# One 512-column product in place of two of 256 in a full expert slot, and a sum behind it

## The chip, the cores and the metric

The kernel runs on one core of one Trainium2 chip. The metric is the device time of one execution in microseconds (us); a measurement is the median of several runs. The engines are TensorE (PE; its weight loads are listed apart as PEld), VectorE (DVE), ScalarE (ACT), GpSimd (POOL) and SyncE (SP). Each works through its own list of instructions in order and waits where a semaphore tells it to.

## What is computed

The reference is a local attention with summary keys, followed by a mixture of experts in which each token goes to the one expert with the largest gate. Only the second part matters here (3072 tokens, width D = 512, E = 8 experts, hidden width F = 1024):

```python
e_idx = np.argmax(x @ w_gate, axis=1)
for e in range(E):
    mask = e_idx == e
    h = np.maximum(x[mask] @ w1[e], 0.0)
    ye = h @ w2[e]
    out[mask] = gate_w[mask, None] * eom[mask, e, None] * ye
```

## The kernel before

**Tiling.** Tokens are gathered by expert into slots of 256 rows (a full slot) or 128 (a half slot). Slot 0 is worked among the last of the attention, slot 1 by `full_with` while DVE still works out the table of the remaining slots, the others by `full` and `half`. There are 11 full slots of the kind that the change touches (slot 1, then seven in a row, then three that alternate with three half slots).

**Precision.** Products run on float32r operands. To keep float32 accuracy, each operand is split into a high part (rounded to float32r) and a low part (the rest), and a product is three: high by high, high weights by low rows, low weights by high rows. ACT makes high parts, DVE subtracts to make low parts. This holds for the weights (`split_w`, L868 and L869, on 128x512 tiles; sixteen tiles of w1 and w2 for each slot), for the rows (`take_x`, L883 and L884) and for the hidden layer (L902 and L903).

**A full slot.** `first(j)`, for j = 0 to 7, makes 128 of the 1024 hidden columns: for each of four chunks c of D, three products of 256 columns into one PSUM tile `hp` (L899 to L901), so 96 products for a slot. ACT then writes `hh`, the high part of relu(hp) (L902), and DVE `hl`, the low part (L903). The PSUM tiles alternate between two tags of two banks each ("S" and "PT"), so `hp` of j+4 reuses the bank of j. `second` makes the output with 48 products of 512 columns (L1082 to L1084, six in each block j); ahead of block 4, `take_x` transposes the rows of the next slot (L881) and splits them (L883, L884). The rows are in `xh` and `xl`, two tiles apart; the weights of the next slot are split into place as soon as the tile that they replace has been used.

**Order.** In the attention and in slot 1 every engine keeps the order in which the program is written (`manual_schedule(engines=ALL)`). In slot 1, each `first(j)` is followed on DVE by up to three small steps of the slot table (`next(rest)`, L728 to L760 and L640 to L688) and by one split of a weight tile; the loop over the second blocks then goes on with splits, and with `take_x` ahead of block 4 (`full_with`, L990 to L1018). From slot 2 on only POOL has the written order; for the others the framework chooses one when the program is built, by its own estimate of times.

Of the kernel before, what the change touches and what calls it, by code (L numbers as in the profile page):

```python
# [11 lines left out]
F32 = mybir.dt.float32  # L12
F32R = mybir.dt.float32r
BF16 = mybir.dt.bfloat16
I32 = mybir.dt.int32
AF = mybir.ActivationFunctionType
ALU = mybir.AluOpType
# [5 lines left out]
P = 128  # L23
# [8 lines left out]
PB = {"S": 2, "PT": 2, "PV": 2, "TR": 1, "MS": 1}  # L32
# [16 lines left out]
NC = DM // P  # L49
NF = F // P  # L50
SLOT = 256
# [209 lines left out]
def attention(tc, const, sa, sb, st, ps, dr, q, k, v, id_sb, c_sb, wg_sb, x_dr, l_dr, rt, moe, table, begin, swap):  # L261
# [240 lines left out]
    def route(b):  # L502
# [15 lines left out]
        yield  # L518
        first = tmp("first", [P, TB])
        nc.vector.tensor_reduce(out=first, in_=fi, axis=AX.X, op=ALU.min)  # L520
        yield
        oh = tmp("oh", sh)
# [246 lines left out]
class Experts:  # L769
# [17 lines left out]
    def open_first(self, pool):  # L787
        self.pool1, self.mp, self.mp2 = pool, pool.__enter__(), None
        self.wt = {1: [self.fixed(self.mp, f"w1{x}", NF, [P, 512], dt) for x, dt in (("h", F32R), ("l", F32))]}
        self.xg = self.fixed(self.mp, "xg", 2, [P, DM], F32)  # L790
        self.xh, self.xl = (self.mp.tile([P, NC, SLOT], dt, name=f"xhl{i}", tag=f"xhl{i}", bufs=1)
                            for i, dt in enumerate((F32, F32R)))
        for t in self.xg:
            self.tc.nc.gpsimd.memset(t, 0.0)
        self.wt[2] = [self.fixed(self.mp, f"w2{x}", NF // 2, [P, 512], F32R) for x in "hl"]

    def open_second(self, pool):
        self.pool2, self.mp2 = pool, pool.__enter__()
        for x, made in zip("hl", self.wt[2]):
            made += self.fixed(self.mp2, f"w2{x}_", NF // 2, [P, 512], F32R)  # L800
# [90 lines left out]
    def first(self, j, hidden, nxt, tag):  # L891

        nc = self.tc.nc
        hh, hl = hidden
        hp = self.ps.tile([P, SLOT], F32, name="hp", tag=tag, bufs=PB[tag])
        fs = slice((j % 4) * P, (j % 4) * P + P)
        for c in range(NC):
            w_h, w_l = (x[4 * (j // 4) + c] for x in self.wt[1])
            nc.tensor.matmul(hp, lhsT=w_h[:, fs], rhs=self.xh[:, c, :], start=c == 0, stop=False)  # L899
            nc.tensor.matmul(hp, lhsT=w_h[:, fs], rhs=self.xl[:, c, :], start=False, stop=False)  # L900
            nc.tensor.matmul(hp, lhsT=w_l[:, fs], rhs=self.xh[:, c, :], start=False, stop=c == NC - 1)  # L901
        nc.scalar.activation(hh[:, j, :], hp, AF.Relu)  # L902
        nc.vector.scalar_tensor_tensor(hl[:, j, :], hp, 0.0, hh[:, j, :].bitcast(F32), ALU.max, ALU.subtract)  # L903
        if j % 4 == 3:
            self.fetch_w(1, nxt, range(j - 3, j + 1))

# [74 lines left out]

    def early_x(self, c):
        if c == 0:
            self.xh = self.mp.tile([P, NC, SLOT], F32R, name="xhl0", tag="xhl0", bufs=1)
        self.take_x(2, (c,))

    def early_write(self):
# [32 lines left out]
    def half(self, s, nxt_n=2):  # L1020
# [31 lines left out]
        with self.tc.manual_schedule(engines={mybir.EngineType.PE}):  # L1052
            first(0, range(4))
            relu(0)
            first(1, range(SPLIT))
            turn(0)
            first(1, range(SPLIT, 4))
            relu(1)
            self.fetch_w(1, nxt, range(4))
            yp.append(ps.tile([P, DM], F32, name="yp0", tag="PV", bufs=PB["PV"]))  # L1060
            for j in range(NF):
                if j == XAT and nxt in self.slots:
                    self.take_x(nxt_n)
                    self.fetch(s + 2, 2)
                self.second_block(j, yp, hh, hl)
                if j == TAT:
                    turn(1)
                    self.fetch_w(1, nxt, range(4, 8))
                if j < NF - 1:
                    if j >= 2:  # L1070
                        self.fetch_w(2, nxt, [j - 2])
                else:
                    with self.tc.manual_schedule(engines={mybir.EngineType.PE, mybir.EngineType.DVE}):
                        self.write(s, yp)
                        self.fetch_w(2, nxt, [j - 2, j - 1, j])
# [110 lines left out]
```

## Time and profile before

| | us |
|---|---|
| median of three runs | 521.12 (520.93 to 524.67) |
| the profiled execution, as a run | 519.98 |
| the profiled execution, its span (first to last instruction) | 517.8 |
| PE busy in that span | 479.9 |
| DVE busy | 363.7 |
| ACT busy | 319.8 |

An engine's busy time is a sum over stages with different limits. A row of a timeline gives the start, the duration, the engine, the line and the tiles; `[0.50 <-ACT hh L902]` at its end says that the engine sat idle for 0.50 us before it, until that instruction was done. Matmuls overlap: a product is listed with some 0.28 us, while the next starts 0.12 us after it. What a product costs is therefore the distance from one start to the next.

### The profile page before, as it was taken

How to read it: one execution, taken by the hardware profiler on the slowest of the kernel's cores; microseconds unless marked ns; L12 is line 12 of the kernel's file. 1: busy time of each engine (PE TensorE's matmuls, PEld its weight loads, DVE VectorE, ACT ScalarE, POOL GpSimd, SP SyncE). 2: the span in 40 equal slices, each digit the busy share in tenths (PEclk: the TensorE clock that was granted, in tenths of full speed). 3: DMA queues.
4: the chain of work that ended last, by engine and by line, in shares of the span. 5: the costliest groups of instructions: out<-in, count | busy, mean ns of one | idle time of the engine just before them, and what ended most of it. 6: DMA issues, size and time to landing. Idle time of an engine off the chain costs nothing.

```text
span 517.8 us, 12814 instructions
## 1 busy us (share of the span) xinstructions
PE 479.9 (93%) x4486; PEld 409.3 (79%) x4486; DVE 363.7 (70%) x802; ACT 319.8 (62%) x633; POOL 229.3 (44%) x257
## 2 busy tenths in 40 slices
PE   6877999979988999999999999999999989989992
PEld 6756677667656788989899898989899869869871
DVE  2748767979886679895757666574757678668674
ACT  3475679577766876555556555463756567567573
POOL 8353556457796615845235131322315315415212
PEclk9997999999999999999999999999999999999998
DMA  9999929999128379728574949476674966967952
GB/s 220 192 231 189 251 67 260 247 255 227 44 86 271 94 221 384 280 72 299 176 268 170 324 137 312 146 265 197 218 237 168 303 207 245 311 209 246 300 193 82
DMA packets 108283, 111.40 MB, mean 215 GB/s; under 512 B 42878, under 2 KB 70110, under 8 KB 108208
## 3 DMA queue, kind: packets, MB, share of 16 engines
q1 hardware_dynamic: 99488, 91.75, 60.1%
q0 software_dynamic: 8720, 18.73, 11.7%
q8 instruction: 37, 0.61, 0.5%
q14 instruction: 38, 0.31, 0.2%
HBM read 98.70 MB, written 15.15 MB: 220 GB/s over the span
## 4 chain that ended last, share of the span: by engine, by line
PE 73%; DVE 6%; ACT 5%; DMA 5%; issue 4%; SPq 3%; POOL 1%; DVEq 0%; ACTq 0%; POOLq 0%
PE yp L1084 9%; PE yp L1083 9%; PE yp L1082 9%; PE hp L901 8%; PE hp L899 8%; PE hp L900 8%; PE pv L447 3%; PE sp L400 3%; PE hp L964 3%; PE pt L432 3%; PE xp L881 2%; PE ms L323 2%; DMA raw<-in_moe_w_dram 2%; DVE pr L410 2%; DMA raw_q<-in_q_dram 2%
## 5 line engine op out<-in xcount | busy, mean ns | idle before, releaser
L869 DVE TENSOR_TENSOR w2l<-raw,w2h 128x512 fp32r<-128x512 f32 x128 | 84.9, 688 | 41.0 <-ACT w2h L868 40.4
L868 ACT ACTIVATE w2h<-raw 128x512 fp32r<-128x512 f32 x128 | 78.0, 628 | 55.8 <-PE yp L1084 23.7
L901 PE MATMUL hp<-xhl,w1l 128*128 128x256 f32 x352 | 99.4, 283 | 0.0
L900 PE MATMUL hp<-xhl,w1h 128*128 128x256 f32 x352 | 99.4, 283 | 0.0
L899 PE MATMUL hp<-xhl,w1h 128*128 128x256 f32 x352 | 99.0, 283 | 0.0
L832 POOL DMA_INDIRECT xg<-x_dr,lst x34 | 40.4, 1188 | 120.0 <-PE xp L881 109.2
L1082 PE MATMUL yp<-w2h,hh 128*128 128x512 f32 x216 | 86.6, 401 | 0.0
L1084 PE MATMUL yp<-w2h,hl 128*128 128x512 f32 x216 | 85.0, 394 | 0.0
L1083 PE MATMUL yp<-w2l,hh 128*128 128x512 f32 x216 | 85.0, 393 | 0.0
L869 DVE TENSOR_TENSOR w1l<-raw,w1h 128x512 fp32r<-128x512 f32 x117 | 75.3, 693 | 8.6 <-ACT w1h L868 7.3
L868 ACT ACTIVATE w1h<-raw 128x512 fp32r<-128x512 f32 x120 | 67.3, 621 | 6.8 <-DMA raw<-in_moe_w_dram 5.2
L900 PEld LDWEIGHTS hp<-xhl,w1h 128*128 128x128 f32 x352 | 67.4, 191 | 0.9
L899 PEld LDWEIGHTS hp<-xhl,w1h 128*128 128x128 f32 x352 | 67.2, 191 | 1.0
L901 PEld LDWEIGHTS hp<-xhl,w1l 128*128 128x128 f32 x352 | 67.4, 192 | 0.0
L902 ACT ACTIVATE hh<-hp 128x256 fp32r<-128x256 f32 x88 | 33.5, 381 | 51.9 <-PE hp L901 49.8
L903 DVE SCALAR_TENSOR_TENSOR hl<-hp,hh 128x256 fp32r<-128x256 f32 x88 | 36.1, 420 | 35.2 <-ACT hh L902 35.1
L422 POOL TENSOR_TENSOR pr<-pr,mn 128x960 f32<-128x960 f32 x24 | 43.4, 1811 | 35.4 <-DVE mn L417 14.2
L1107 POOL DMA_INDIRECT out_dram<-y,lst x27 | 31.3, 1159 | 56.7 <-DVE y L1104 29.2
L1084 PEld LDWEIGHTS yp<-w2h,hl 128*128 128x128 f32 x216 | 40.5, 188 | 8.8
L1082 PEld LDWEIGHTS yp<-w2h,hh 128*128 128x128 f32 x216 | 40.7, 188 | 8.1
L1083 PEld LDWEIGHTS yp<-w2l,hh 128*128 128x128 f32 x216 | 40.7, 188 | 7.8
L278 ACT ACTIVATE pT<-pt 120x512 f32<-120x512 f32 x48 | 27.2, 595 | 26.7 <-PE pt L432 26.5
(202 smaller groups left out, 843.3 us busy)
## 6 DMA issues: line engine op xcount, KB each, us to landing
raw<-in_moe_w_dram SPq DMA_DIRECT2D x248, 256.0 KB, 5.1
raw_k<-in_k_dram SPq DMA_DIRECT2D x12, 512.0 KB, 7.9
raw_q<-in_q_dram SPq DMA_DIRECT2D x12, 512.0 KB, 5.5
vw<-in_v_dram SPq DMA_DIRECT2D x44, 128.0 KB, 6.5
x_dr<-xs POOLq DMA_DIRECT2D x17, 256.0 KB, 4.3
vw<-in_v_dram SPq DMA_DIRECT2D x33, 64.0 KB, 4.5
w1l<-in_moe_w_dram SPq DMA_DIRECT2D x8, 256.0 KB, 3.4
x_dr<-xs SPq DMA_DIRECT2D x7, 256.0 KB, 3.9
```

What stands on the lines that cost most here:

```text
L422: nc.gpsimd.tensor_tensor(pr, pr, mns.pop(i).unsqueeze(2).to_broadcast([P, H, W]), ALU.subtract)
L832: nc.gpsimd.indirect_dma_start(out=self.xg[t], out_offset=None, in_=self.x_dr[0:rows, :], in_offset=bass.IndirectOffsetOnAxis(ap=self.list ...
L868: nc.scalar.activation(hi, raw, AF.Copy)
L869: (lo_by or nc.vector).tensor_tensor(lo, raw, hi.bitcast(F32), ALU.subtract)
L899: nc.tensor.matmul(hp, lhsT=w_h[:, fs], rhs=self.xh[:, c, :], start=c == 0, stop=False)
L900: nc.tensor.matmul(hp, lhsT=w_h[:, fs], rhs=self.xl[:, c, :], start=False, stop=False)
L901: nc.tensor.matmul(hp, lhsT=w_l[:, fs], rhs=self.xh[:, c, :], start=False, stop=c == NC - 1)
L902: nc.scalar.activation(hh[:, j, :], hp, AF.Relu)
L903: nc.vector.scalar_tensor_tensor(hl[:, j, :], hp, 0.0, hh[:, j, :].bitcast(F32), ALU.max, ALU.subtract)
L1082: nc.tensor.matmul(y, lhsT=hh[:, j, tk], rhs=w_h, start=j == 0, stop=False)
L1083: nc.tensor.matmul(y, lhsT=hh[:, j, tk], rhs=w_l, start=False, stop=False)
L1084: nc.tensor.matmul(y, lhsT=hl[:, j, tk], rhs=w_h, start=False, stop=j == NF - 1)
```

## The change

In a full slot the rows' high and low parts lie side by side in one tile (`x[:, c, 0, :]` and `x[:, c, 1, :]`), and the high weights meet both in one product of 512 columns, which fills the whole bank: half 0 collects high by high, half 1 high weights by low rows. The product of the low weights with the high rows (256 columns) is added to half 1. The bank's halves are then added: ACT copies half 1 to a new SBUF tile `lo`, DVE adds half 0 to it, and the relu (ACT) and the subtraction (DVE) read `lo` instead of PSUM. The written order (`first`, then the table's steps, then the split) is not changed. Slot 0 and the half slots keep their products.

```diff
-        self.xh, self.xl = (self.mp.tile([P, NC, SLOT], dt, name=f"xhl{i}", tag=f"xhl{i}", bufs=1)
-                            for i, dt in enumerate((F32, F32R)))
+        self.rows(F32)
...
+    def rows(self, dt):
+        self.x = self.mp.tile([P, NC, 2, SLOT], dt, name="xhl", tag="xhl", bufs=1)
+        self.xh, self.xl = self.x[:, :, 0, :], self.x[:, :, 1, :]
...
-        hp = self.ps.tile([P, SLOT], F32, name="hp", tag=tag, bufs=PB[tag])
+        hp = self.ps.tile([P, 2, SLOT], F32, name="hp", tag=tag, bufs=PB[tag])
...
-            nc.tensor.matmul(hp, lhsT=w_h[:, fs], rhs=self.xh[:, c, :], start=c == 0, stop=False)
-            nc.tensor.matmul(hp, lhsT=w_h[:, fs], rhs=self.xl[:, c, :], start=False, stop=False)
-            nc.tensor.matmul(hp, lhsT=w_l[:, fs], rhs=self.xh[:, c, :], start=False, stop=c == NC - 1)
-        nc.scalar.activation(hh[:, j, :], hp, AF.Relu)
-        nc.vector.scalar_tensor_tensor(hl[:, j, :], hp, 0.0, hh[:, j, :].bitcast(F32), ALU.max, ALU.subtract)
+            nc.tensor.matmul(hp.rearrange("p a n -> p (a n)"), lhsT=w_h[:, fs], rhs=self.x[:, c].rearrange("p a n -> p (a n)"),
+                             start=c == 0, stop=False)
+            nc.tensor.matmul(hp[:, 1, :], lhsT=w_l[:, fs], rhs=self.xh[:, c, :], start=False, stop=c == NC - 1)
+        lo = self.mp2.tile([P, SLOT], F32, name="lo", bufs=2)
+        nc.scalar.activation(lo, hp[:, 1, :], AF.Copy)
+        nc.vector.tensor_tensor(lo, hp[:, 0, :], lo, ALU.add)
+        nc.scalar.activation(hh[:, j, :], lo, AF.Relu)
+        nc.vector.scalar_tensor_tensor(hl[:, j, :], lo, 0.0, hh[:, j, :].bitcast(F32), ALU.max, ALU.subtract)
...
-            self.xh = self.mp.tile([P, NC, SLOT], F32R, name="xhl0", tag="xhl0", bufs=1)
+            self.rows(F32R)
```

## Rows read from the trace of the kernel before

**Rows 1.** The page's first part: busy time of each engine, its share of the span, and its instructions.

```profile
PE 479.9 (93%) x4486; PEld 409.3 (79%) x4486; DVE 363.7 (70%) x802; ACT 319.8 (62%) x633; POOL 229.3 (44%) x257
```

**Rows 2.** Busy time of each engine by stretch: slot 1's first stage, its second stage, and six full slots in a row. Columns: the stretch, its length, busy time of PE, PEld, DVE, ACT and POOL with the number of instructions, the granted clock, the share of the DMA engines, GB/s.

```profile
207.20:218.70 11.50, 11.50 (x97) 11.50 (x96) 9.99 (x51) 5.98 (x13) 9.55 (x17) 1.00 0.79 295
218.70:230.67 11.97, 11.97 (x59) 9.86 (x57) 11.83 (x28) 7.64 (x14) 6.58 (x9) 1.00 0.34 94
...
254.50:395.10 140.60, 140.60 (x911) 127.78 (x910) 89.90 (x162) 79.96 (x162) 39.45 (x36) 1.00 0.65 221
```

**Rows 3.** Everything that PE waited for from 195 us to the end: us in total, times, the longest.

```profile
PE ht L1046 <- ACT h L1041: 4.3, 3, 1.9
```

**Rows 4.** PE's timeline in one full slot. The first two rows are the first and the last of 84 products of 256 columns in a row; the next two the first and last of 17 of 512 columns; the last two the first and last of 23 of 512 columns, behind the transposes.

```profile
301.15 0.28 PE L899 MATMUL hp<-xhl,w1h 128*128 128x256 f32 x1
...
311.10 0.28 PE L901 MATMUL hp<-xhl,w1l 128*128 128x256 f32 x1
...
314.27 0.40 PE L1083 MATMUL yp<-w2l,hh 128*128 128x512 f32 x1
...
317.92 0.40 PE L1084 MATMUL yp<-w2h,hl 128*128 128x512 f32 x1
...
319.27 0.40 PE L1083 MATMUL yp<-w2l,hh 128*128 128x512 f32 x1
...
324.41 0.40 PE L1084 MATMUL yp<-w2h,hl 128*128 128x512 f32 x1
```

**Rows 5.** Groups of instructions by line, forms kept apart: busy us and mean ns of one, then the idle time before them. The tiles that stand for PSUM are hp, lp, pv, xtr and xp; raw is in SBUF.

```profile
L868 ACT ACTIVATE w1h<-raw 128x512 fp32r<-128x512 f32 x120 | 67.3, 621 | 6.8 <-DMA raw<-in_moe_w_dram 5.2 <-PE hp L900 1.5
...
L903 DVE SCALAR_TENSOR_TENSOR hl<-hp,hh 128x256 fp32r<-128x256 f32 x88 | 36.1, 420 | 35.2 <-ACT hh L902 35.1
L902 ACT ACTIVATE hh<-hp 128x256 fp32r<-128x256 f32 x88 | 33.5, 381 | 51.9 <-PE hp L901 49.8 <-DVE w2l L869 0.8
...
L460 DVE TENSOR_TENSOR xs<-pv,den 128x256 f32<-128x256 f32 x48 | 18.1, 420 | 0.8
L884 DVE TENSOR_TENSOR xhl<-xp,xhl 128x512 fp32r<-128x512 f32 x27 | 17.4, 682 | 0.0
...
L278 ACT ACTIVATE xT<-xtr 128x512 f32<-128x512 f32 x24 | 14.3, 596 | 5.2 <-PE xtr L471 5.1
...
L278 ACT ACTIVATE ls<-lp 128x256 f32<-128x256 f32 x12 | 4.6, 383 | 1.2 <-PE lp L482 0.8 <-issue 0.3
```

**Rows 6.** ACT's timeline in slot 1: the relu of j = 0 and of j = 7, the splits behind it, and the high part of slot 2's rows.

```profile
208.89 0.39 ACT L902 ACTIVATE hh<-hp 128x256 fp32r<-128x256 f32 x1 [0.80 <-PE hp L901]
...
218.91 0.39 ACT L902 ACTIVATE hh<-hp 128x256 fp32r<-128x256 f32 x1 [0.54 <-PE hp L901]
219.19 2.18 ACT L868 ACTIVATE w1h<-raw 128x512 fp32r<-128x512 f32 x4
221.27 1.14 ACT L868 ACTIVATE w2h<-raw 128x512 fp32r<-128x512 f32 x2
...
224.91 1.07 ACT L883 ACTIVATE xhl<-xp 128x512 fp32r<-128x512 f32 x2
```

**Rows 7.** DVE's timeline in slot 1: the subtraction of j = 0 and the small step behind it, those of j = 3 and j = 7, and the low part of slot 2's rows.

```profile
209.30 0.42 DVE L903 SCALAR_TENSOR_TENSOR hl<-hp,hh 128x256 fp32r<-128x256 f32 x1 [0.50 <-ACT hh L902]
209.65 0.15 DVE L728 SCALAR_TENSOR_TENSOR r_rest<-early,c_sb 128x8 f32<-128x8 f32 x1
...
213.56 0.42 DVE L903 SCALAR_TENSOR_TENSOR hl<-hp,hh 128x256 fp32r<-128x256 f32 x1 [0.29 <-ACT hh L902]
...
223.11 0.42 DVE L903 SCALAR_TENSOR_TENSOR hl<-hp,hh 128x256 fp32r<-128x256 f32 x1
...
228.91 1.27 DVE L884 TENSOR_TENSOR xhl<-xp,xhl 128x512 fp32r<-128x512 f32 x2
```

**Rows 8.** All that DVE waited for between 207 and 232 us: us in total, times, the longest.

```profile
DVE hl L903 <- ACT hh L902: 0.8, 2, 0.5
DVE w2l L869 <- ACT w2h L868: 0.5, 1, 0.5
```

**Rows 9.** PE's timeline at the end of slot 1: the first product of its last block that reads `hl`, and the first products of slot 2.

```profile
229.73 0.40 PE L1084 MATMUL yp<-w2h,hl 128*128 128x512 f32 x1
...
230.67 0.63 PE L899 MATMUL hp<-xhl,w1h 128*128 128x256 f32 x4
```

**Rows 10.** The granted clock where it fell. First PE's last product of the kernel, then stretches with the columns of Rows 2 (the clock is the third number from the end).

```profile
507.36 0.40 PE L1084 MATMUL yp<-w2h,hl 128*128 128x512 f32 x1
...
512.00:513.00 1.00, 0.00 (x0) 0.00 (x0) 0.00 (x0) 0.00 (x0) 0.00 (x0) 0.83 0.15 37
...
41.00:42.00 1.00, 0.00 (x0) 0.00 (x0) 1.00 (x2) 0.41 (x2) 1.00 (x2) 0.81 1.38 143
42.00:44.00 2.00, 1.15 (x22) 1.15 (x24) 1.97 (x2) 0.00 (x0) 1.69 (x2) 0.50 1.41 162
...
48.00:49.00 1.00, 1.00 (x7) 0.79 (x5) 0.93 (x5) 0.70 (x2) 0.00 (x0) 0.77 1.16 195
```

**Rows 11.** What DVE waited for in the six slots from 254.5 to 395 us: us in total, times, the longest.

```profile
DVE w2l L869 <- ACT w2h L868: 24.2, 21, 3.9
DVE hl L903 <- ACT hh L902: 22.0, 24, 1.0
DVE y L1104 <- PE yp L1084: 3.9, 6, 0.7
```

## The prediction

> **What bounds the kernel now.** I read the page's busy times first [rows 1]: PE is the busiest engine, at 93% of the span. Then the waits of PE alone, from 195 us on, where the slots begin: it waited 4.3 us in all, each time in a half slot, never in a full one [rows 3]. Then the busy times by stretch [rows 2]: in six full slots PE is busy for all of the 140.6 us while DVE has 89.9 and ACT 80.0, or 15.0 and 13.3 us in a slot of 23.4. So in the full slots the distance between PE's products sets the time, and DVE and ACT have some 8 and 10 us free in each. The first two rows of the same group show one exception: in slot 1, DVE is busy for 9.99 of 11.50 and then 11.83 of 11.97 us. It has the table's small steps there besides the splits, in a written order. PE does not wait for it yet. So there are two questions: what PE saves in each slot, and whether slot 1 can bear more work on DVE.
>
> **What PE saves.** For each j and chunk, two products of 256 columns become one of 512; the third stays. In a full slot 84 products of 256 columns start within 9.95 us, 119.9 ns apart (83 distances) [rows 4]. Products of 512 columns are 228.1 ns apart (3.65 us over 16) ahead of the transposes and 233.6 ns (5.14 over 22) behind them. I see nothing in the rows that says which of the two the new product gets, so I take their middle, 230.9. Two old products cost 239.8, so the change saves 8.9 ns on each of 32 pairs, 0.28 us in a slot: bounds 0.20 (at 233.6) and 0.37 (at 228.1). The columns streamed are the same 3072 for each j; what is saved is only the part of each product that does not grow with its columns. No row has 512 and 256 columns alternating, so I also keep a floor of no saving at all.
>
> At 2.4 GHz, the granted clock's upper level, which these stretches have, 256 columns take 106.7 ns and 512 take 213.3, so each product here carries about 13 to 20 ns on top [rows 4]. The Trainium skill ("TensorE: Matmul & The Clock Gate", section "Wait — 56ns, not 53.3ns?") puts that fixed part at about 2.5 ns. By it the change would save 0.08 us in a slot, an estimate from that page, and the sum below would end 2.0 us later; the rows differ from it, and I go by the rows.
>
> **What ACT and DVE pay.** For each j ACT gets one more instruction and DVE one more. ACT's copy of half 1, PSUM to SBUF with 128x256, has its like in `ls<-lp`: 383 ns. DVE's add, one operand from PSUM, has its like in `xs<-pv,den`: 420 ns. The relu now reads SBUF; at 512 columns ACT takes 621 ns from SBUF against 596 from PSUM, so I put it at 0.38 + 0.02 = 0.40 us. The subtraction stays at 420 ns [rows 5]. That is about 0.40 us on ACT and 0.42 on DVE for each j. But the order matters more than the work: copy (ACT), add (DVE), relu (ACT), subtract (DVE) is a chain. Where the order is as written, add and subtract are neighbours on DVE, and DVE stands idle while ACT makes the relu between them. Handing over costs little: in j = 0 the relu ends at 208.89 + 0.39 = 209.28, and the subtraction starts at 209.30 [rows 6, 7]. So where DVE is the late engine, each j costs it 0.42 (add) + 0.02 + 0.40 (relu) + 0.02 = 0.86 us more.
>
> **In slots 2 and later** I cost this at nothing: DVE goes from 15.0 to at most 15.0 + 8 x 0.86 = 21.9 us in a slot of 23.2, ACT from 13.3 to 16.5. What hides it are DVE's waits of today, 50.1 us in six slots, or 8.4 in each [rows 11]. `hl` of the last j is wanted only by the last block of the second stage, and a bank of `hp` only four j later. If that cover were gone it would be rival C.
>
> **In slot 1** there is no such cover. Between 207 and 232 us DVE waited 1.3 us in all, of it 0.8 for the relu: 0.50 in j = 0 and 0.29 in j = 3 [rows 7, 8]. The 0.50 remains (the chain begins with ACT as before); the 0.29 is swallowed. DVE falls behind by 8 x 0.86 - 0.3 = 6.6 us by the end of j = 7. Banks don't stop PE meanwhile: by j = 3 the delay is 3 x 0.86 = 2.6 us, so its add ends by 213.56 + 0.42 + 2.6 = 216.6 [rows 7], and PE wants that bank for j = 7, at 207.20 + 7 x 1.40 = 217.0 (1.40 us being twelve times 119.9 ns less the saving) [rows 2, 4]. From the subtraction of j = 7, which starts at 223.11, DVE works without a gap to the low part of slot 2's rows at 228.91 [rows 7, 8]; the splits ahead of that are eight, and ACT, held up behind its own relu, delivers one each 0.54 us (2.18 for four) [rows 6], faster than DVE takes them. So the whole delay reaches `xl`: its first half is ready at 228.91 + 0.68 + 6.6 = 236.2 instead of 229.6 [rows 5, 7]. What is late next is PE. Its last block reads `hl` of j = 7, ready at 223.11 + 0.42 + 6.6 = 230.1, so it stalls there for under 1 us, is done near 231.1, and then cannot begin slot 2, for the new first product reads both halves of the rows. Slot 2 begins at 236.2 instead of 230.67 [rows 9]: **5.5 us later**, after an idle time of 5.1 us. Bounds: 8 x 0.42 - 0.8 = 2.6 us of delay if DVE could use the time of the relu, which leaves 229.6 + 2.6 - 230.67 = 1.5; and 6.6 + 0.8 for slower chains, which gives 6.3.
>
> Behind `take_x`, POOL's gathers for slot 3 and SP's loads wait for the table's last steps on DVE and come as much later, with PE as late as they are: nothing more is lost.
>
> **Edits that cost nothing.** The joint tile for the rows is taken anew when slot 1's rows come; slot 0's products have read the old one by then. 32 weight loads fewer in a slot lie under the products anyway.
>
> **The sum.** What slot 1 saves is lost in its stall; the ten full slots behind it save 10 x 0.28 = 2.8 us (2.0 to 3.7). Against the profiled execution: 519.98 (span 517.8 and 2.2 around it) + 5.5 - 2.8 = 522.7. It lies 1.1 below the median of the runs, so on the median's scale 521.12 + 2.7 = **523.8 us**.
>
> **Rivals.**
> A. *The clock falls in the stall.* After PE's last product (507.36 + 0.40) the granted clock held until two thirds of the microsecond 512 to 513 (0.83 in that row), 4.9 us of idleness; my stall has 5.1. Earlier it fell at 41.6 after sparse work, and came back only in 48 to 49, some 5.6 us after PE resumed at 42.85 [rows 10]. Products at 1.2 GHz for that long lose half of it: 2.8 us more, **526.6**. For it: the idle times are alike. Against it: in the row the engine fell only at the very end of such a time. The Trainium skill ("TensorE: Matmul & The Clock Gate", section "Why this matters for your kernels") warns of idle gaps between bursts of products; the rows show such a fall twice.
> B. *No stall.* DVE's small steps have gaps between them that an idle engine could use, or the order is not as I read it: 521.12 - 11 x 0.28 = **518.0**. Against it: DVE's 11.83 of 11.97 us [rows 2].
> C. *DVE starves PE in every slot*, the case that ends slower for certain. It decides if the order chosen for slots 2 and later keeps add and subtract neighbours and if DVE keeps more than 23.2 - 21.9 = 1.3 us of its 8.4 us of waits. If it keeps 2.2, a slot costs 24.1, 0.7 more than today's 23.4: 521.12 + 5.5 + 10 x 0.7 = **533.6**. For it: half of those waits are for w2's high parts, which PE's blocks release [rows 11]. Against it: such waits shrink when DVE is late.
> D. *The new product hides its own overhead* and costs what its columns take, 213.3: 26.5 ns saved on each pair, 0.85 us in a slot: with the stall 521.12 + 5.5 - 8.5 = **518.1**; without it 521.12 - 9.3 = **511.8**. Against it: products of 512 columns with longer cover for their weights don't do so today [rows 4].
> E. *No saving*: 523.8 + 2.8 = **526.6**.
>
> **Chances.** Forecast 0.42; A 0.22; B 0.14; C 0.10; D 0.07 (half of it without the stall); E 0.05. The range from 518.0 to 528.0 leaves out C and part of D; the forecast's own range is 519 to 525.5 (bounds of stall and saving together: 521.12 + 1.5 - 3.7 and + 6.3 - 2.0). About 1% (5.2 us) is what a measurement of this kernel can tell from no change: under 515.9 only D without the stall, 0.04; over 526.3 C, E, and most of A, 0.28; the rest 0.68.
>
> **What would show it.** In the changed profile: products of 512 and 256 columns with 231 and 120 ns behind them, and slots of some 23.2 us; in slot 1 the add and the subtraction 0.44 us apart on DVE, with a wait for ACT between; `xl` of slot 2 near 236 and a PE wait for it of about 5 us, with the granted clock at 1.00 behind it (at 0.50 for A); no PE wait in the slots behind. I am wrong if PE begins slot 2 before 232, if PE waits in the later full slots, or if a pair saves more than 12 ns.

## The result, and the profile after

The changed kernel takes 528.83 us (median of six runs, 525.58 to 530.85) where the kernel before has 521.21 beside it: a ratio of 1.013, with an interval of 1.010 to 1.016. In a second group of runs it takes 527.71 against 521.55: 1.011, 1.008 to 1.014. So it is slower by a little over 1%, and my 523.8 was 4 to 5 us too low; the upper end of my range, 528.0, lies between the two medians. In three of the five groups of runs the kernel before, too, took some 540 us, and the traces of those groups have pauses of several us in slot 1 for which the profile records no releaser ("outside pauses" below), in kernels with the old slot 1 too; so runs are compared within their group.

The profiled execution took 530.85 us, with a span of 528.8. Busy times first; they answer to [rows 1].

```profile
PE 485.7 (92%) x4134; PEld 395.7 (75%) x4134; DVE 390.7 (74%) x890; ACT 346.4 (66%) x721; POOL 231.4 (44%) x257
```

PE lost 352 instructions (32 for each of 11 slots), DVE and ACT gained 88 each. Next, slot 1's first stage, slot 1's second stage with the time until slot 2 begins, and six full slots; columns as in [rows 2].

```profile
210.95:222.05 11.10, 11.10 (x66) 9.78 (x65) 8.11 (x40) 4.87 (x12) 9.34 (x15) 1.00 0.85 311
222.05:239.97 17.92, 12.48 (x58) 9.35 (x57) 15.61 (x47) 10.50 (x23) 8.05 (x11) 0.96 0.20 63
271.31:410.51 139.20, 139.20 (x722) 117.74 (x721) 104.60 (x209) 92.49 (x208) 41.76 (x39) 1.00 0.65 227
```

The first and third stretches are shorter than before. In the six full slots PE is busy throughout, 139.20 us against 140.60, and DVE at 104.60 is still far from full. The loss is in the second row: 17.92 us against 11.97, with PE idle for 5.4 of them. What PE waited for, as in [rows 3]:

```profile
PE hp L902 <- DVE xhl L887: 4.8, 1, 4.8
PE yp L1088 <- ACT hh L1055: 2.5, 3, 1.1
PE yp L1088 <- ACT hh L908: 0.7, 1, 0.7
```

The first row is new: one wait of 4.8 us for the low part of slot 2's rows. PE's timeline around it answers to [rows 9].

```profile
233.56 0.50 PE L1088 MATMUL yp<-w2h,hh 128*128 128x512 f32 x1 [0.69 <-ACT hh L908]
...
234.83 0.39 PE L1090 MATMUL yp<-w2h,hl 128*128 128x512 f32 x1
239.97 0.79 PE L902 MATMUL hp<-xhl,w1h 128*128 128x512 f32 x1 [4.75 <-DVE xhl L887]
```

DVE's timeline in slot 1, answering to [rows 7]: j = 0, the add and subtraction of j = 7, and the low part of slot 2's rows; then all its waits in slot 1, as in [rows 8] (a third, of 0.3 us, lies just ahead of slot 1).

```profile
212.95 0.42 DVE L907 TENSOR_TENSOR lo<-hp,lo 128x256 f32<-128x256 f32 x1 [0.61 <-ACT lo L906]
213.86 0.42 DVE L909 SCALAR_TENSOR_TENSOR hl<-lo,hh 128x256 fp32r<-128x256 f32 x1 [0.48 <-ACT hh L908]
...
232.64 0.42 DVE L907 TENSOR_TENSOR lo<-hp,lo 128x256 f32<-128x256 f32 x1
233.54 0.42 DVE L909 SCALAR_TENSOR_TENSOR hl<-lo,hh 128x256 fp32r<-128x256 f32 x1 [0.48 <-ACT hh L908]
...
239.24 1.28 DVE L887 TENSOR_TENSOR xhl<-xp,xhl 128x512 fp32r<-128x512 f32 x2
```

```profile
DVE hl L909 <- ACT hh L908: 3.9, 8, 0.5
DVE lo L907 <- ACT lo L906: 0.6, 1, 0.6
```

In every j the add and the subtraction start 0.90 us apart, and DVE stands idle for 0.48 of that until ACT's relu is done: eight times 0.48 is the 3.9 us of the waits. Measured from slot 1's start, the subtraction of j = 7 comes at 22.59 us (before: 15.91) and the low part of the rows at 28.29 (before: 21.71): the delay of 6.6 us reaches it whole. What it is made of shows in the stretch from slot 1's start to the low part of the rows, before and after (columns as in [rows 2]):

```profile
207.20:228.91 21.71, 21.71 (x146) 19.96 (x145) 20.06 (x76) 12.98 (x26) 16.13 (x25) 1.00 0.58 200
210.95:239.24 28.29, 23.58 (x121) 19.13 (x119) 22.99 (x84) 14.64 (x34) 17.39 (x25) 0.99 0.45 158
```

DVE works 2.9 us more (22.99 against 20.06, eight adds) and stands idle 3.65 us more (5.30 against 1.65).

The granted clock, in the columns of [rows 10], during the wait and behind it:

```profile
237.00:238.00 1.00, 0.00 (x0) 0.00 (x0) 1.00 (x2) 1.00 (x3) 0.73 (x1) 1.00 1.01 257
238.00:239.00 1.00, 0.00 (x0) 0.00 (x0) 1.00 (x3) 1.00 (x3) 0.00 (x0) 0.76 0.87 327
239.00:240.00 1.00, 0.03 (x1) 0.03 (x1) 1.00 (x3) 1.00 (x3) 0.00 (x0) 0.50 0.56 203
240.00:244.00 4.00, 4.00 (x13) 3.42 (x14) 3.58 (x6) 1.28 (x3) 0.14 (x1) 0.50 0.17 56
244.00:245.00 1.00, 1.00 (x4) 0.85 (x4) 0.00 (x0) 0.36 (x1) 0.89 (x1) 0.50 0.80 266
245.00:246.00 1.00, 1.00 (x6) 0.86 (x5) 0.70 (x2) 0.90 (x2) 0.81 (x1) 0.83 0.67 258
```

It fell to the lower level (1.2 GHz) within 238 to 239, near 238.5, some 3.3 us after PE's last product (234.83 + 0.39), and came back near 245.3. From 239.97 to 245.3 products ran at half speed: 5.35 us of which half, 2.7, is lost.

The groups of the new evacuation, against [rows 5], and the pitch of a full slot: the first and the last transposes in a row of four slots, of the kernel before and then of the changed one.

```profile
L909 DVE SCALAR_TENSOR_TENSOR hl<-lo,hh 128x256 fp32r<-128x256 f32 x88 | 36.1, 420 | 9.6 <-ACT hh L908 8.8
L907 DVE TENSOR_TENSOR lo<-hp,lo 128x256 f32<-128x256 f32 x88 | 36.0, 418 | 8.6 <-ACT lo L906 6.1 <-issue 2.0
L908 ACT ACTIVATE hh<-lo 128x256 fp32r<-128x256 f32 x88 | 35.5, 414 | 27.5 <-DVE lo L907 27.2
L906 ACT ACTIVATE lo<-hp 128x256 f32<-128x256 f32 x88 | 32.8, 374 | 12.5 <-PE hp L904 8.2 <-DVE hl L909 4.1
```

```profile
271.17 1.03 PE L881 MATMUL xp<-id_sb,xg 128*128 128x128 f32 x8
...
365.14 1.04 PE L881 MATMUL xp<-id_sb,xg 128*128 128x128 f32 x8
```

```profile
271.31 1.04 PE L884 MATMUL xp<-id_sb,xg 128*128 128x128 f32 x8
...
364.11 1.03 PE L884 MATMUL xp<-id_sb,xg 128*128 128x128 f32 x8
```

Four slots take 92.80 us, 23.20 each; before, they take 93.97 and 23.49. A slot saves 0.29 us.

Where the whole span went, in us, for the traces that have no outside pause (the columns are told in the experiments). A slot counts from its first product, and the tail is what lies behind the start of PE's last product:

| stretch | before | after | after again | slot 1 as before | PE kept busy | other order |
|---|---|---|---|---|---|---|
| to slot 1 | 207.20 | 210.95 | 210.67 | 209.34 | 208.70 | 208.13 |
| slot 1 to slot 2 | 23.47 | 29.02 | 29.05 | 23.47 | 29.04 | 24.89 |
| slots 2 to 9 | 187.49 | 187.28 | 186.64 | 184.55 | 184.55 | 186.15 |
| half slot 1 to half slot 3 | 75.56 | 74.29 | 74.66 | 75.08 | 75.22 | 74.45 |
| half slot 3 to PE's last product | 13.64 | 14.75 | 13.98 | 15.50 | 14.91 | 13.49 |
| tail | 10.44 | 12.51 | 12.40 | 10.46 | 12.28 | 12.19 |

The first row lies ahead of the new products and of the new evacuation, and still has 3.75 us of the 11.0 between the two profiled executions. Up to slot 1 the kernels of the five columns on the right are the same, and their traces differ by 2.8 us there (208.13 to 210.95); the one trace of before lies 0.9 us under the lowest of them. The tail had me look for a cause in the new evacuation, but it varies by itself: kernels traced twice gave 13.10 and 10.46 (slot 1 as before), 10.45 and 12.19 (only slot 1 changed), and 10.08 and 12.40 (the last order below). So neither row is shown to be the change's. What it did is in rows 2 and 3: 5.55 us lost, and eight slots that should save 2.3 end up 0.2 shorter.

### The profile page after: what moved, and what is told of

It is laid out like the page before. It is cut to its first block, busy times and chain, and to the rows that moved or that the text cites. A ratio compares the mean times of both kernels' runs of the same rounds, so it can differ in the third digit from the quotient of the medians.

```text
span 528.8 us, 12288 instructions
## 1 busy us (share of the span) xinstructions
PE 485.7 (92%) x4134; PEld 395.7 (75%) x4134; DVE 390.7 (74%) x890; ACT 346.4 (66%) x721; POOL 231.4 (44%) x257
## 4 chain that ended last, share of the span: by engine, by line
PE 66%; DVE 10%; ACT 7%; DMA 7%; issue 4%; SPq 3%; POOL 2%; ACTq 0%; DVEq 0%; POOLq 0%
PE hp L902 15%; PE yp L1090 8%; PE yp L1088 8%; PE yp L1089 8%; PE hp L904 7%; PE hp L970 3%; PE pv L447 3%; PE sp L400 3%; PE pt L432 2%; DMA raw_q<-in_q_dram 2%; SPq L316 2%; DMA raw<-in_moe_w_dram 2%; PE xp L884 2%; DVE pr L410 2%; PE xtr L471 1%
## 5 line engine op out<-in xcount | busy, mean ns | idle before, releaser
L902 PE MATMUL hp<-xhl,w1h 128*128 128x512 f32 x352 | 128.0, 402 | 4.8 <-DVE xhl L887 4.8
L1090 PE MATMUL yp<-w2h,hl 128*128 128x512 f32 x216 | 83.1, 398 | 0.3
L902 PEld LDWEIGHTS hp<-xhl,w1h 128*128 128x128 f32 x352 | 67.1, 191 | 20.4 <-DVE xhl L887 5.2
L1113 POOL DMA_INDIRECT out_dram<-y,lst x27 | 33.3, 1234 | 101.6 <-DVE y L1110 89.8
L871 ACT ACTIVATE w1h<-raw 128x512 fp32r<-128x512 f32 x120 | 69.3, 622 | 11.5 <-PE hp L902 5.6
L908 ACT ACTIVATE hh<-lo 128x256 fp32r<-128x256 f32 x88 | 35.5, 414 | 27.5 <-DVE lo L907 27.2
L410 DVE TENSOR_TENSOR pr<-sp,c_sb 128x480 f32<-128x480 f32 x48 | 29.2, 649 | 21.8 <-PE sp L400 18.4
L909 DVE SCALAR_TENSOR_TENSOR hl<-lo,hh 128x256 fp32r<-128x256 f32 x88 | 36.1, 420 | 9.6 <-ACT hh L908 8.8
L907 DVE TENSOR_TENSOR lo<-hp,lo 128x256 f32<-128x256 f32 x88 | 36.0, 418 | 8.6 <-ACT lo L906 6.1
```

Source lines behind the costliest of these rows:

```text
L410: nc.vector.tensor_tensor(pr[:, x], sp[x][:, :, 0:W], c_sb[:, m:m + W].unsqueeze(1).to_broadcast([P, HP, W]), ALU.add)
L871: nc.scalar.activation(hi, raw, AF.Copy)
L902: nc.tensor.matmul(hp.rearrange("p a n -> p (a n)"), lhsT=w_h[:, fs], rhs=self.x[:, c].rearrange("p a n -> p (a n)"), start=c == 0, stop=F ...
L907: nc.vector.tensor_tensor(lo, hp[:, 0, :], lo, ALU.add)
L909: nc.vector.scalar_tensor_tensor(hl[:, j, :], lo, 0.0, hh[:, j, :].bitcast(F32), ALU.max, ALU.subtract)
L1090: nc.tensor.matmul(y, lhsT=hl[:, j, tk], rhs=w_h, start=False, stop=j == NF - 1)
```

## The experiments

**The changed kernel again, and slot 1 as before.** Theory: DVE's fixed order in slot 1 makes the stall, the stall lowers the clock, the other slots only gain. Rival: the later slots and the end lose. In the second kernel, slot 1 calls the old `first` under another name; all else stays changed.

```diff
...
-            self.first(j, hidden, None, "S" if j % 2 else "PT")
+            self.first_three(j, hidden, None, "S" if j % 2 else "PT")
```

> The changed kernel again, beside the experiments of this group, so that they can be set against it on one chip. Theory (slot 1's stall of 5.5 us, some 2.4 us of products at the lower clock behind it, 0.29 us saved in each of ten full slots, some 2 us more at the end): 528.8 us where the kernel before has 521.2, a ratio of 1.015. From the start of slot 1 to that of slot 2: 29.0 us against 23.5.

> Slot 1 has its old three products and its old evacuation, the other ten full slots the new ones; on a chip where slot 1 has no other stall. Theory (the loss is slot 1's stall and the clock behind it): slot 2 begins 23.5 us after slot 1, the clock stays at 1.00, ten slots save 2.9 us, and the end costs some 1.9 more as in the changed kernel (halves -1.3, last half +1.1, tail +2.1): 521.2 - 2.9 + 1.9 = 520.2, a ratio of 0.998 to before and 8.6 us under the changed kernel. Rival (the loss lies in the later full slots and the end): the same as the changed kernel within 2 us, 527 to 529.

Measured: 527.71 us for the changed kernel (1.011, 1.008 to 1.014) and 519.89 for the one with slot 1 as before (0.998, 0.995 to 1.001). The waits of PE from 195 us on, of the second kernel:

```profile
PE yp L1104 <- ACT hh L1071: 3.8, 3, 1.5
```

and its span from slot 1 to slot 2, and behind it (columns as in [rows 2]):

```profile
209.34:232.81 23.47, 23.47 (x153) 21.35 (x152) 21.70 (x79) 13.62 (x27) 18.20 (x25) 1.00 0.56 197
232.81:240.00 7.19, 7.19 (x43) 6.32 (x42) 5.56 (x11) 5.03 (x11) 4.35 (x5) 1.00 0.60 193
```

The wait for the rows is gone, PE is busy throughout, and the clock stays up. The two medians differ by 7.8 us; the traces give 29.05 - 23.47 = 5.6 for the stall and 186.64 - 184.55 = 2.1 behind it, 7.7 together. The changed kernel's second trace has the fall of the clock earlier than the first; its last product of slot 1 and its clock:

```profile
234.58 0.39 PE L1090 MATMUL yp<-w2h,hl 128*128 128x512 f32 x1
239.72 0.79 PE L902 MATMUL hp<-xhl,w1h 128*128 128x512 f32 x1 [4.75 <-DVE xhl L887]
```

```profile
237.00:238.00 1.00, 0.00 (x0) 0.00 (x0) 1.00 (x3) 1.00 (x3) 0.48 (x1) 0.58 0.93 257
...
243.00:244.00 1.00, 1.00 (x5) 0.90 (x4) 0.33 (x1) 0.00 (x0) 0.39 (x1) 0.51 0.71 236
244.00:245.00 1.00, 1.00 (x7) 0.87 (x7) 0.06 (x1) 0.72 (x2) 0.69 (x2) 1.00 0.79 283
```

It fell near 237.2, 2.2 us after PE was done (234.97), and was back at 244.0: 4.3 us of products at half speed, 2.1 us lost, as the table's third row has it. So slot 1 carries the loss, and the ten later slots do not lose. Whether they win is not certain: eight of them take 2.9 us less (187.49 - 184.55), but the median lies only 1.7 under that of before, within its interval.

The same kernel had been run before in a group with the outside pauses:

> Slot 1 alone goes back to three products of 256 columns and to the relu and subtraction from PSUM; all other full slots keep the change. Theory (slot 1's written order costs a stall of 5.5 us and, with the clock's fall in it, 2.4 more, while each later full slot saves 0.28): no PE wait at the start of slot 2, granted clock 1.00 there, 518.4 to 520.6 us. Rival (the loss sits in the later slots, whose order the framework chooses anew, and in the half slots): 525 us or more, with PE waits behind slot 2.

Measured: 539.4 against 538.78, 1.001 (0.998 to 1.004). Its slot 1, with the old order, took 35.8 us up to slot 2 instead of 23.5, with waits for which nothing is recorded, so it told nothing.

**PE kept busy in the stall.** Is the time behind the stall the clock's? Behind slot 1's last block PE makes 80 products that nobody reads.

```diff
+        hm = self.ps.tile([P, P], F32, name="warmer2", tag="S", bufs=PB["S"])
+        for _ in range(80):
+            self.tc.nc.tensor.matmul(hm, lhsT=self.rt["ones"], rhs=self.rt["ones"], start=True, stop=True)
```

> The changed kernel, and behind slot 1's last block PE makes 80 products of 128 columns of a constant, which nobody reads, while it would stand idle. Theory (4.7 us of slot 2's first products ran at 1.2 GHz because PE had stood still): the clock stays at 1.00 when slot 2 begins, slot 2 begins no later than in the changed kernel (29.0 us after slot 1), and slots 2 to 4 take 2.4 us less: 526.4. Rival (the clock falls for some other reason, or what it costs is hidden because DVE and ACT are late there anyway): the same time as the changed kernel, 528.8, or more.

Measured: 527.35 us, 1.010 (1.006 to 1.015). PE's timeline, and the clock at the start of slot 2, where it was 0.50 in the changed kernel:

```profile
232.83 4.64 PE L1022 MATMUL warmer<-ones 128*128 128x128 bf16 x80
237.74 0.50 PE L902 MATMUL hp<-xhl,w1h 128*128 128x512 f32 x1 [0.27 <-DVE xhl L887]
```

```profile
237.00:238.00 1.00, 0.73 (x10) 0.56 (x8) 1.00 (x3) 1.00 (x3) 0.00 (x0) 1.00 0.37 123
238.00:239.00 1.00, 1.00 (x7) 0.87 (x7) 1.00 (x3) 1.00 (x2) 0.00 (x0) 1.00 0.02 6
```

Slot 2 begins as late as in the changed kernel (29.04 us after slot 1), the clock stays at 1.00, and slots 2 to 9 take 184.55 us, the same as without a stall: the 2.1 to 2.7 us behind the stall are the clock's. The median of the whole doesn't show this: 0.4 us under the changed kernel, with six runs between 522.4 and 529.6. I ran it again:

> The changed kernel with 80 unread products in the stall once more: in the first run of it the clock stayed at 1.00 and the stretch from slot 2 to the first half slot took 184.6 us instead of 186.6 to 187.3, but the median of six runs, 527.4, lay only 0.4 under the changed kernel's, with a spread of 7 us. Theory (the clock costs what that stretch shows): 2.1 to 2.4 us under the changed kernel's ratio of 1.011 to 1.013, so 1.006 to 1.009. Rival (what the clock gives back is lost again at the half slots, where weights are waited for): 1.010 or more.

Measured: 540.51 against 539.97, 1.003 (0.998 to 1.007), in a group with the outside pauses; slots 2 to 9 took 184.79. The ratio lies under what either theory expected, so it decides nothing. The stretch says the same twice; the price in the whole time is not separated from the spread.

**The sum alone, and the products alone.** The first keeps three products of 256 columns, one into half 0 and two into half 1, with the whole new evacuation; the second has the wide product but leaves out the sum: `hh` and `hl` are made from half 0 as before, so the parts in half 1 are missing from its output.

```diff
-            nc.tensor.matmul(hp.rearrange("p a n -> p (a n)"), lhsT=w_h[:, fs], rhs=self.x[:, c].rearrange("p a n -> p (a n)"),
-                             start=c == 0, stop=False)
+            nc.tensor.matmul(hp[:, 0, :], lhsT=w_h[:, fs], rhs=self.xh[:, c, :], start=c == 0, stop=False)
+            nc.tensor.matmul(hp[:, 1, :], lhsT=w_h[:, fs], rhs=self.xl[:, c, :], start=False, stop=False)
```

```diff
-        lo = self.mp2.tile([P, SLOT], F32, name="lo", bufs=2)
-        nc.scalar.activation(lo, hp[:, 1, :], AF.Copy)
-        nc.vector.tensor_tensor(lo, hp[:, 0, :], lo, ALU.add)
-        nc.scalar.activation(hh[:, j, :], lo, AF.Relu)
-        nc.vector.scalar_tensor_tensor(hl[:, j, :], lo, 0.0, hh[:, j, :].bitcast(F32), ALU.max, ALU.subtract)
+        nc.scalar.activation(hh[:, j, :], hp[:, 0, :], AF.Relu)
+        nc.vector.scalar_tensor_tensor(hl[:, j, :], hp[:, 0, :], 0.0, hh[:, j, :].bitcast(F32), ALU.max, ALU.subtract)
```

> Every full slot keeps three products of 256 columns, the first into half 0 and the two others into half 1, and has the new chain of copy, add, relu and subtraction: the cost of the sum without the saving of the wider product. Theory: 96 products 120 ns apart in a slot again, stall and clock as in the changed kernel, so 2.8 to 3.1 us above it: 531.8 us. Rival (the wider product saves nothing as a whole, since PE waits for ACT and DVE elsewhere): as the changed kernel, 528.8 us.

> The wide product everywhere, but the sum is left out: relu and subtraction read half 0 alone, from PSUM, as before (the low parts of the hidden layer's input are dropped). ACT and DVE then have their old work. Theory: no stall, eleven slots that save 0.28 each: 521.2 - 3.1 = 518.1 us. Rival (the wider product does not save, or the order that the framework chooses anew costs as much): 521 us or more.

Measured, with before at 538.78: the sum alone 547.19, 1.019 (1.014 to 1.023); the products alone 532.68, 0.990 (0.985 to 0.995). Transposes four slots apart, of the sum alone and then of the products alone:

```profile
297.95 1.04 PE L884 MATMUL xp<-id_sb,xg 128*128 128x128 f32 x8
...
391.92 1.03 PE L884 MATMUL xp<-id_sb,xg 128*128 128x128 f32 x8
```

```profile
312.44 1.04 PE L884 MATMUL xp<-id_sb,xg 128*128 128x128 f32 x8
...
404.94 1.03 PE L884 MATMUL xp<-id_sb,xg 128*128 128x128 f32 x8
```

93.97 us, exactly as before: with the old products the sum costs nothing in the later slots. 92.50 us: the products save 0.37 in a slot, 0.08 more than with the sum. Over all of slots 2 to 9 that difference is not seen: 184.70 us for the products alone, 184.55 for the kernel with the sum and slot 1 as before. The 0.990 of the products alone lies under the expected 0.994 (518.1 of 521.2), which its interval still holds; its slot 1 took 30.5 us up to slot 2, where the kernel with the old slot 1 took 35.8 in the same group, so it lost less to the outside pauses. The 1.019 of the sum alone fits a loss in slot 1 and no saving, but the next kernel, run in the same group and almost the same by theory, has 1.002 (its twelve runs lie between 534.1 and 546.2 us); from slot 2 to the first half slot their traces agree (190.8 and 190.5 us), so I lean on the slots' lengths and not on these three ratios.

**The change in slot 1 alone,** the mirror image: `full` calls the old three products, `full_with` the new ones.

```diff
...
-            self.first(j, hidden, s + 1, "S" if j % 2 else "PT")
+            self.first_three(j, hidden, s + 1, "S" if j % 2 else "PT")
```

> The change in slot 1 alone; the later full slots keep three products of 256 columns and the old relu and subtraction. Theory: the stall ahead of slot 2 and the clock's fall are all there and nothing is saved behind them: 521.2 + 5.5 + 2.4 = 529 us, above the changed kernel by up to 2. Rival (the loss sits in the later slots): 523 us or less.

> The mirror image of the run with three products in slot 1: only slot 1 has the change, the ten full slots behind it have the old three products and the old evacuation. Theory (slot 1's stall costs 5.6 us and the clock behind it 2.1 to 2.4; the later slots only save): 521.5 + 7.8 = 529.3, a ratio of 1.015, with slot 2 29.0 us after slot 1 and 23.5 us for each later full slot. Rival (part of the loss comes from the later slots' new evacuation): under 526.

Measured, both times in groups with the outside pauses: 1.002 (0.998 to 1.007) and 1.010 (1.005 to 1.014). The first settles nothing. The second shows a loss from slot 1 alone, though under the 1.015 expected, as it would be if the pauses gave DVE part of its time back (argued, not shown). PE's first products of slot 2 there:

```profile
253.26 0.74 PE L921 MATMUL hp<-xhl,w1h 128*128 128x256 f32 x4 [2.72 <-ACT xhl L886]
255.03 0.58 PE L922 MATMUL hp<-xhl,w1h 128*128 128x256 f32 x1 [1.03 <-DVE xhl L887]
```

Two waits, 3.75 us together, for the two parts of the rows, and the clock at 0.50 from 256 to 258.

**Other orders in slot 1.** If it is the order, the change can stay and the order be mended. First the subtraction is written behind the table's steps and the split of its j, and slot 2's rows are taken ahead of block 2, not 4. In the second kernel the relu moves behind the split too.

```diff
-        nc.vector.scalar_tensor_tensor(hl[:, j, :], lo, 0.0, hh[:, j, :].bitcast(F32), ALU.max, ALU.subtract)
+
+        def subtract():
+            nc.vector.scalar_tensor_tensor(hl[:, j, :], lo, 0.0, hh[:, j, :].bitcast(F32), ALU.max, ALU.subtract)
...
             self.split(EARLY_V, "v")
+            subtract()
...
-            if j == 4:
+            if j == 2:
```

> All of the change stays, and only slot 1's written order differs: the subtraction for hl stands behind the table's steps and the weight split of its j instead of ahead of them, so that DVE does these while ACT makes the relu; and the rows of slot 2 are taken ahead of block 2 of the second stage instead of block 4. Theory (the stall is DVE's wait for the relu in a fixed order): DVE loses some 0.42 us for each j instead of 0.86, xl is ready before PE is done, slot 2 begins some 23.2 us after slot 1, and the clock stays at 1.00: 528.8 - 5.8 - 2.4 = 520.6, level with before. Rival (DVE's work in slot 1 is too much in any order): slot 2 begins 26 us or more after slot 1, and the time is 524 or more.

Measured: 522.86 us, 1.002 (0.999 to 1.004). What PE waited for from 190 us on, and what DVE waited for in slot 1:

```profile
PE hp L902 <- DVE xhl L887: 1.6, 1, 1.6
PE yp L1095 <- ACT hh L1062: 1.6, 2, 1.0
PE hp L902 <- DVE lo L907: 1.1, 1, 1.1
```

```profile
DVE w1l L872 <- ACT w1h L871: 1.5, 3, 0.6
DVE lo L907 <- ACT lo L906: 0.6, 1, 0.6
```

All eight waits for the relu are gone, and 4.8 us under the changed kernel are gained with the same work on every engine. The stall is 1.6 us, the clock keeps 1.00. The run has two edits in one, and its trace tells them apart. The stretch from slot 1's start to the low part of slot 2's rows, to be set beside the two above:

```profile
208.13:232.28 24.15, 23.25 (x121) 19.43 (x119) 20.97 (x81) 12.91 (x30) 17.35 (x25) 1.00 0.45 160
```

It is 4.1 us shorter than in the changed kernel. DVE is idle for 3.2 us in it instead of 5.3, which the order gave; the other 2.0 are work (20.97 against 22.99, three instructions fewer), put behind the rows by taking them earlier. So the order alone is not shown to remove the stall. The expected 520.6 is missed, and DVE now waits for ACT's splits (1.5 us), which stand behind the relu in ACT's order. Hence the second kernel, here against the one just shown:

```diff
-        nc.scalar.activation(hh[:, j, :], lo, AF.Relu)
...
-        def subtract():
+        def relu_and_subtract():
+            nc.scalar.activation(hh[:, j, :], lo, AF.Relu)
...
-            subtract()
+            relu_and_subtract()
```

> As the run with the subtraction put off and the rows taken early, but ACT's relu too stands behind the weight split of its j: ACT writes copy, split, relu; DVE writes add, table steps, split, subtraction. There a ring of add, relu, ACT's split, DVE's split and subtraction took 2.36 us for each of the last j (0.42 + 0.42 + 0.62 + 0.69 + 0.42 = 2.57 less overlaps), DVE waited 1.5 us for ACT's splits in it, PE waited 1.6 us for xl and 1.1 us for a lo in slot 2. Theory (it was the ring, not DVE's own work): DVE's waits for ACT's splits in slot 1 go, xl is ready some 1.5 us earlier, slot 2 begins 23.3 to 23.6 us after slot 1, PE's waits of 2.7 us fall to under 0.8: 522.9 - 2.2 = 520.7, a ratio of 0.998 to before. Rival (DVE's own work, one add more for each j, sets it): nothing changes, 24.9 us and 522.9.

> The last order once more (relu, weight split and subtraction of slot 1 put so that neither DVE nor ACT waits for the other), because the first run of it fell on executions of some 540 us, in which slot 1 has pauses of 6 us that no change of this study makes, in the kernel before as well. Theory: on executions of some 521 us slot 2 begins 23.3 to 23.6 us after slot 1, the clock stays at 1.00, ten slots save 0.29 us each, the half slots and the end give back 1 to 2 of it: 519 to 521, a ratio of 0.995 to 0.999. Rival (DVE's own work sets slot 1 in any order): 24.9 us from slot 1 to slot 2, and 1.002 as with the other order.

Measured, both times in groups with the outside pauses: 536.83 against 539.97, 0.994 (0.990 to 0.999), and 535.43 against 540.66, 0.993 (0.988 to 0.997). PE's waits from 190 us on in the second:

```profile
PE hp L902 <- issue: 5.9, 2, 5.4
PE hp L902 <- DVE lo L907: 2.5, 2, 1.4
PE yp L1095 <- ACT hh L1062: 2.5, 3, 1.1
```

No wait for slot 2's rows is left; the first row is the outside pause. In both groups this version is faster than the kernel before, by 0.6% and 0.7%; the changed kernel did not run in them. It had no run among executions of 521 us, so its 23.3 to 23.6 us from slot 1 to slot 2 stay unconfirmed.

## Why the prediction was half right

- **The stall in slot 1: right.** Forecast: DVE 6.6 us late, slot 2 begins 29.0 us after slot 1 (236.2 - 207.20). Measured 6.6 and 29.02. That it is so exact is in part luck: the relu and its handing over took 0.48 us instead of 0.44, so DVE's idle time grew by 3.65 us where 8 x 0.44 - 0.3 = 3.2 was forecast, and its work by 2.9 where I had 8 x 0.42 = 3.4. The two errors cancel. Rival B, no stall, is out.
- **The saving in a full slot: right in size.** 0.29 us against 0.28. In slot 1, where wide and narrow products alternate without others between them, 32 pairs take 11.10 us, 346.9 ns a pair: 12.8 ns under three times 119.9: 1.1 over my upper bound, and over the 12 at which I called myself wrong. Times 32 that would be 0.41 in a slot; four later slots kept 0.29 of it each, and 0.37 without the sum. Over slots 2 to 9 without a stall the saving is 2.9 us, 0.6 more than eight times 0.29. Why, the runs do not say. Rivals D and E are out.
- **DVE in the later slots: right.** In the changed kernel PE waits in no full slot there, and the sum alone leaves the slot at 23.49 us. Rival C is out.
- **The clock: the step that failed.** I had the stall at 5.1 us and gave its fall (rival A) only 0.22, because in [rows 10] the clock had held for 4.9 us of idleness. It fell near 238.5 here, 3.3 us after the last product, and near 237.2, 2.2 us after it, in the second trace. One row showed one moment of a fall, not how early it can come; I used it as if it were a threshold. The ends of the other traces show the spread: behind the kernel's last product the fall came 2.0 us later at the earliest (only slot 1 changed, first trace) and 5.1 us at the latest (the changed kernel). The price, 2.7 and 2.1 us, is that of rival A (2.8). The Trainium skill ("TensorE: Matmul & The Clock Gate", section "Why this matters for your kernels") warns of such gaps; these runs agree with it for 4.75 us of idleness, and the gaps of 1.64 and 1.09 us in the other order left the clock at 1.00.
- **What is left.** With the clock in, the sum is 521.1 + 5.5 + 2.1 to 2.7 - 2.8 = 525.9 to 526.5, and 526.6 stood there as rival A's. Some 1 to 3 us up to 527.7 and 528.8 are not located. Part of it is that I let the last two full slots save 0.6: from the first half slot to PE's last product, before took 89.2 us, and the five traces with the new evacuation there 87.9 to 90.6, so nothing is seen to be saved between the half slots, where PE waits for ACT in every kernel.

## What to carry to other kernels

Where an engine's order is written out, an instruction pair with another engine's step between them costs the engine that step's whole time, each time (here 0.48 us, eight times); count the chain beside the work (here 3.65 us of idle time and 2.9 of work on DVE), and put other work between the two. A stall on PE has a second price, the clock behind it, and one gap that it survived does not bound when it falls. A saving of some 1% in each of ten slots (2.9 us) is worth less than one stall at the one place without slack (5.6 us, and 2.1 to 2.7 for the clock).

## What the runs showed of the hardware

- The time from PE's last product to the fall of the granted clock was 2.2 and 3.3 us in two traces of the changed kernel's stall, and 2.0 to 5.1 us at the ends of the fourteen traces (4.9 in [rows 10]); after products resumed it was back in 4.3 and 5.35 us (and 5.6 in [rows 10]).
- One program's tail behind PE's last product took 10.1 us in one execution and 12.4 in another, and the attention ahead of slot 1 differed by up to 2.8 us in five traces whose program is the same up to there.
- In three groups the kernel before took 539 to 541 us instead of 521. Traces there show PE, DVE and ACT in slot 1 waiting up to 5.4, 7.1 and 8.7 us at a time with no releaser recorded on the core. The cause is open.
